# Transposing k once, copying its exchanged halves, and moving sums and loads between engines in a scheduled attention and feed-forward kernel

## The chip, the cores and the metric

One Trainium2 chip, one core. The engines are TensorE (PE; its weight loads are shown apart as PEld), VectorE (DVE), ScalarE (ACT), GpSimd (POOL) and SyncE (SP, which only issues transfers). The metric is device time of one execution in microseconds. The median of three timed executions of the kernel before is 986.57 us (986.48, 986.57, 989.59).

## The reference

Block-causal attention (8 batches, 8 heads, 576 positions of 64, blocks of 64: a position sees its own block and all earlier ones), then a feed-forward layer on its output:

```python
scores = scale * np.matmul(q, k.transpose(0, 1, 3, 2))
mask = block_i >= block_j
scores = np.where(mask, scores, -1000000000.0)
attn = np.exp(scores - np.max(scores, axis=-1, keepdims=True))
attn = attn / (np.sum(attn, axis=-1, keepdims=True) + 1e-09)
out = np.matmul(attn, v)
h = x @ w_in                      # x: 4608 x 512, w_in: 512 x 2048
g = h * np.clip(h + 3.0, 0.0, 6.0) / 6.0
return g @ w_out                  # w_out: 2048 x 512
```

Inputs and outputs are float32.

## The kernel before

Work is split into 32 pairs of heads (n = 0 to 31, four to a batch) and 13 pieces of positions for the feed-forward layer (up to 384 columns, 16 hidden tiles each). The first four pairs and the first piece are computed in f32 (names ending in 32, h0, o0), while the weights are loaded, scaled and split. From pair 4 on every f32 operand is split into two f16 parts, hi and lo, scaled by powers of two; a product is then three f16 products, hi hi, hi lo and lo hi, except for scores, where all parts of q meet all of k.

For scores, `qk_prep` takes a pair's q and k (positions on partitions), finds their maxima (`qkmx`), from these a power-of-two scale (`rs_q`, by way of a small matmul `mb_q`), writes scaled hi parts and residues into `qks`, and one transposing transfer on SyncE's queue turns `qks` into `qkT` (head dimension on partitions). `qkT` has three planes: plane 0 has q's hi on the lower 64 partitions and lo on the upper; planes 1 and 2 have k arranged so that the two products of plane 0 with each add up to all four combinations. In the kernel before, plane 1 holds k's hi on both halves and plane 2 its lo on both, so hi and lo are each written twice into `qks` (the second time by a copy that may run on VectorE, GpSimd or ScalarE) and three planes of nine 128-wide blocks are transposed: twenty-seven blocks.

`s_group` does the scores of three blocks of rows (groups g = 0, 1, 2): matmuls `s`, maxima `st`, exponentials `p` on ScalarE, normalised hi and lo parts `phl`, and transposing transfers `pT<-phl` on SyncE (8 blocks for group 0, 18 for group 1, 8, 8 and 10 for group 2). `pv_group` (two per pair) multiplies `pT` by v's parts `vhl` and writes piece buffers `x`. Then `ffn1_` gives hidden tiles h (two PSUM banks; in the last two pieces by products `m` of sums of halves), r and g, and `ffn2_` accumulates o; `osb` is stored.

The order is not that of the code: a recorder takes every operation with the engines that may run it, and a list scheduler (`schedule`) places them by a due time (`key`), estimated durations (`cost`), buffers, and two tables of numbers: `SHIFT` moves due times and `LEAN` moves the choice between engines. All recorded instructions therefore carry one line, L852, and are told apart by tiles. Each engine runs its list in order and waits where an operand is late. Loads may go on SyncE's or ScalarE's queue (`AQ`); stores and transposing transfers go on SyncE's. `pv_group32` spreads reciprocal row sums over a diagonal (`rd`), one block at a time.

Of the kernel before, what the change touches and what calls it, by code (L numbers as in the profile page):

```python
# [8 lines left out]
F16 = mybir.dt.float16  # L9
BF16 = mybir.dt.bfloat16  # L10
# [41 lines left out]
QKA = 8  # L52
RDW = "PA"
# [369 lines left out]
class Recorder:  # L423
# [165 lines left out]
    def cost(self, eng, method, args, kw, outs, ins):  # L589
# [40 lines left out]
        if eng == "gpsimd":  # L630
            if method == "memset":
                return 20 + 1.0 * n, 50 + n, False
            occ = 75 + (2.0 if method == "tensor_tensor" else 1.1) * n
            return occ, occ + 30, True
# [1479 lines left out]
```

## Time and profile before

| | |
|---|---|
| median of three executions | 986.57 us |
| profiled execution | 993.96 us |
| its span, first to last instruction | 992.2 us |
| mean granted TensorE clock | 0.994 |
| TensorE busy | 969.3 us (98%) |
| weight loads busy | 699.9 us (71%) |
| VectorE busy | 882.7 us (89%) |
| ScalarE busy | 637.2 us (64%) |
| GpSimd busy | 68.4 us (7%) |
| mean DMA rate | 130 GB/s, 129.03 MB |

In the rows, the columns of the stretch table are: stretch and its length, busy time and instruction count of PE, PEld, DVE, ACT and POOL, granted TensorE clock, DMA share and GB/s. Waits read "who waited <- for whom: us in total, times, longest". Timeline rows give start, duration, engine, operation, tiles (written <- read), count, and in brackets idle time before with what ended it; ACTq and SPq are the engine's issuing of a transfer. A tile's rows give minimum/median/maximum duration in ns, first and last start, and the time from issue to landing of its transfers. Group rows end with busy us, mean ns, and idle time before.

### The profile page before, as it was taken

How to read it: one execution, taken by the hardware profiler on the slowest of the kernel's cores; microseconds unless marked ns; L12 is line 12 of the kernel's file. 1: busy time of each engine (PE TensorE's matmuls, PEld its weight loads, DVE VectorE, ACT ScalarE, POOL GpSimd, SP SyncE). 2: the span in 40 equal slices, each digit the busy share in tenths (PEclk: the TensorE clock that was granted, in tenths of full speed). 3: DMA queues.
4: the chain of work that ended last, by engine and by line, in shares of the span. 5: the costliest groups of instructions: out<-in, count | busy, mean ns of one | idle time of the engine just before them, and what ended most of it. 6: DMA issues, size and time to landing. Idle time of an engine off the chain costs nothing.

```text
span 992.2 us, 31091 instructions
## 1 busy us (share of the span) xinstructions
PE 969.3 (98%) x12585; PEld 699.9 (71%) x12585; DVE 882.7 (89%) x2443; ACT 637.2 (64%) x1539; POOL 68.4 (7%) x237
## 2 busy tenths in 40 slices
PE   6999999999999999999999989999999999999998
PEld 5666667777778776687666767777767666768785
DVE  6999999999999999999997968988988879987864
ACT  4788868676767775887785756664757644443422
POOL 1132200000000000000000000000000100000000
PEclk9999999999999999999999989999999999999999
DMA  8974468989969779998996876584877462000000
GB/s 235 314 214 146 97 122 150 177 135 189 180 101 211 139 150 177 158 187 151 172 174 111 136 143 122 105 171 100 130 147 107 84 125 36 2 34 2 34 3 32
DMA packets 407184, 129.03 MB, mean 130 GB/s; under 512 B 393984, under 2 KB 396544, under 8 KB 407040
## 3 DMA queue, kind: packets, MB, share of 16 engines
q1 hardware_dynamic: 351232, 107.26, 57.8%
q10 hardware_dynamic: 55808, 19.78, 8.9%
q8 instruction: 98, 1.61, 0.7%
q14 instruction: 46, 0.38, 0.1%
HBM read 45.09 MB, written 9.44 MB: 55 GB/s over the span
## 4 chain that ended last, share of the span: by engine, by line
PE 51%; ACTq 1%; DVE 1%; ACT 1%; issue 0%
PE o L852 23%; PE h L852 16%; PE m L852 6%; PE s L852 3%; PE pv L852 3%; ACTq L852 1%; ACT osb L852 0%; DVE qks L852 0%; ACT p L852 0%; DVE st L852 0%; DVE x L852 0%; ACT r L852 0%; DVE r L852 0%; DVE osb L852 0%; DVE g L852 0%
## 5 line engine op out<-in xcount | busy, mean ns | idle before, releaser
L852 PE MATMUL o<-wout,g 128*64 128x512 f16 (+3 forms) x3336 | 405.2, 379 | 0.0
L852 PE MATMUL h<-x,win 128*64 128x384 f16 (+2 forms) x3952 | 357.8, 320 | 2.6 <-DVE r L852 2.0
L852 PEld LDWEIGHTS <-win 128*64 128x64 f16 (+1 forms) x4440 | 258.3, 110 | 74.0 <-issue 5.7
L852 PEld LDWEIGHTS <-g 128*64 128x64 f16 x3360 | 206.7, 110 | 119.5 <-issue 1.4
L852 ACT ACTIVATE p<-s,st,esc 128x384 f32<-128x384 f32 (+4 forms) x280 | 163.3, 588 | 61.1 <-DVE st L852 38.0
L852 ACT ACTIVATE r<-h,eg,sh 128x384 f32<-128x384 f32 (+1 forms) x192 | 111.5, 600 | 73.8 <-PE h L852 61.8
L852 DVE SCALAR_TENSOR_TENSOR phl<-p,st,phl 128x384 f16<-128x384 f32 (+4 forms) x252 | 137.1, 586 | 0.2
L852 DVE TENSOR_REDUCE st<-s 128x1 f32<-128x384 f32 (+4 forms) x280 | 117.9, 446 | 11.8 <-PE s L852 11.5
L852 DVE SCALAR_TENSOR_TENSOR r<-r,eg,h 128x384 f32<-128x384 f32 (+1 forms) x160 | 93.0, 585 | 19.6 <-ACT r L852 19.0
L852 DVE SCALAR_TENSOR_TENSOR g<-r,g 128x384 f16<-128x384 f32 (+1 forms) x192 | 101.2, 533 | 9.1 <-ACT g L852 8.2
L852 ACT ACTIVATE g<-r 128x384 f16<-128x384 f32 (+1 forms) x140 | 70.5, 506 | 57.3 <-PE o L852 27.8
L852 PE MATMUL s<-qkT 128*64 128x512 f16 (+7 forms) x1120 | 98.1, 289 | 4.4 <-ACT p L852 4.3
L852 ACT ACTIVATE phl<-p,st 128x384 f16<-128x384 f32 (+4 forms) x149 | 78.5, 567 | 36.3 <-DVE st L852 21.0
L852 PEld LDWEIGHTS <-qkT 128*64 128x64 f16 x1120 | 60.0, 111 | 28.7 <-issue 7.6
L852 PEld LDWEIGHTS <-vhl 128*64 128x64 f16 x1680 | 71.9, 110 | 10.0 <-issue 1.5
L852 PE MATMUL pv<-pT,vhl 128*64 128x192 f16 (+2 forms) x1680 | 72.9, 233 | 0.9 <-DVE x L852 0.5
L852 POOL MEMSET p<- 128x64 f32 x140 | 22.3, 159 | 546.5 <-DVE phl L852 482.9
L852 ACT ACTIVATION_READ_ACCUMULATOR p<-s,st,esc 128x1 f32 x280 | 55.4, 198 | 0.0
L852 ACT ACTIVATE r<-hf,eg,sh 128x192 f32<-128x192 f32 (+1 forms) x48 | 26.2, 592 | 44.0 <-DVE hf L852 42.5
L852 DVE SCALAR_TENSOR_TENSOR qks<-qk,rs_q,qks 128x576 f16<-128x576 f32 x56 | 44.4, 807 | 0.1
L852 DVE TENSOR_SCALAR phl<-p,st 128x128 f16<-128x128 f32 (+4 forms) x103 | 40.1, 414 | 1.0
L852 PE MATMUL m<-x,ws 128*64 128x192 f16 x768 | 37.9, 246 | 0.0
(191 smaller groups left out, 1028.9 us busy)
## 6 DMA issues: line engine op xcount, KB each, us to landing
out_dram<-osb SPq DMA_DIRECT2D x34, 256.0 KB, 2.4
qk<-in_q_dram SPq DMA_DIRECT2D x20, 288.0 KB, 4.8
vnat<-in_v_dram ACTq DMA_DIRECT2D x42, 128.0 KB, 4.2
rawo<-in_moe_w_out_dram SPq DMA_DIRECT2D x9, 512.0 KB, 6.1
qk<-in_k_dram ACTq DMA_DIRECT2D x16, 288.0 KB, 5.7
qk<-in_k_dram SPq DMA_DIRECT2D x12, 288.0 KB, 4.2
vnat<-in_v_dram SPq DMA_DIRECT2D x22, 128.0 KB, 3.5
x<-in_moe_w_in_dram SPq DMA_DIRECT2D x5, 512.0 KB, 7.2
```

The source lines that it names most:

```text
L852: getattr(eng, method)(*args, **kw)
```

## The change

- `qk_prep`: k is written as two halves (lo below, hi above) and transposed as one plane, so `qks` has two planes and the transposition eighteen blocks. Plane 2 of `qkT` is then plane 1 with its halves exchanged, made by two transfers from one half of the partitions to the other on SyncE's queue. The two copies into `qks` fall away.
- `QKA` goes from 8 to 32: for every pair ScalarE may give the scale's input, as two sums of absolute values, where VectorE gives one pass of maxima. (`VMG = 99` leaves the same choice for v off.)
- `RDW`: the three spreadings of a group's row sums become one operation of 192 columns, on VectorE or GpSimd instead of GpSimd or ScalarE.
- Loads of v, q and k from the ninth pair on (`n < 2 * NPAIR` no longer holds) go only on SyncE's queue.
- `cost`: estimated GpSimd durations are raised; both tables have new numbers throughout.

```diff
--- before.py
+++ after.py
@@ -49,8 +49,9 @@
 BQ = ("sync", "scalar")
 OQ = ("sync",)
 GRM = 3
-QKA = 8
-RDW = "PA"
+QKA = 32
+RDW = ("vector", "gpsimd")
+VMG = 99
 
 NMIN = 64
 LANES = 8
@@ -76,324 +77,306 @@
 
 
 SHIFT = {
-    0: 41, 2: 284, 3: -222, 4: 16, 5: -43, 6: -115, 7: 119, 8: 168, 11: -88, 12: 152, 13: 20, 14: -246,
...
+    0: -73, 2: 127, 3: -91, 4: 197, 5: 202, 6: -33, 7: 232, 8: -21, 11: 71, 12: 190, 13: 80, 14: 82, 15: 150,
...
 }
 LEAN = {
-    20: (-1038, 0), 50: (1191, 0), 60: (179, 0), 70: (-42, 0), 80: (0, -166), 110: (-195, 0), 111: (-195, 0),
...
+    20: (154, 0), 21: (49, 0), 50: (307, 0), 80: (0, 17), 81: (403, 0), 111: (68, 0), 140: (-69, 0),
...
 }
 
 
@@ -630,7 +613,7 @@
         if eng == "gpsimd":
             if method == "memset":
                 return 20 + 1.0 * n, 50 + n, False
-            occ = 75 + (2.0 if method == "tensor_tensor" else 1.1) * n
+            occ = 75 + (2.6 if method == "tensor_tensor" else 1.3) * n
             return occ, occ + 30, True
         f32 = mybir.dt.size(ins[0].dtype) == 4
         occ = max(n / 2.37, 26) * (4 if f32 else 1) + 2
@@ -1154,10 +1137,12 @@
         full = (NJ - 1) * P
         for h in range(2):
             nc.load(
-                t[:, :NJ - 1, h, :], v[b, 2 * hp + h, :full].rearrange("(j p) d -> p j d", p=P), AQ
+                t[:, :NJ - 1, h, :], v[b, 2 * hp + h, :full].rearrange("(j p) d -> p j d", p=P),
+                AQ if n < 2 * NPAIR else OQ,
             )
         nc.load(
-            t[:BLK, NJ - 1, :, :], v[b, 2 * hp:2 * hp + 2, full:].rearrange("h p d -> p h d"), AQ
+            t[:BLK, NJ - 1, :, :], v[b, 2 * hp:2 * hp + 2, full:].rearrange("h p d -> p h d"),
+            AQ if n < 2 * NPAIR else OQ,
         )
 
     def v_max(n):
@@ -1168,7 +1153,13 @@
             ab = ab[:, :NJ * 2 * D].rearrange("p (j h d) -> p j h d", h=2, d=D)
             nc.scalar.activation(ab, vnat[n % NVB], AF.Abs, accum_out=vmax[b][:, hp:hp + 1])
         else:
-            absmax(vmax[b][:, hp:hp + 1], vnat[n % NVB], AX.XYZ)
+            ways = [("vector", "tensor_reduce", (vmax[b][:, hp:hp + 1], vnat[n % NVB]),
+                     dict(axis=AX.XYZ, op=ALU.max, apply_absolute_value=True))]
+            if n >= VMG:
+                ab = sm.tile([P, NJ, 2, D], BF16, tag="vs", bufs=1, name=f"va{n}")
+                ways.append(("scalar", "activation", (ab, vnat[n % NVB], AF.Abs),
+                             dict(accum_out=vmax[b][:, hp:hp + 1])))
+            nc.add(ways)
         if hp == NPAIR - 1:
             m1 = sm.tile([P, 1], F32, tag="vm1", name=f"vm1_{b}")
             nc.vector.tensor_reduce(m1, vmax[b], axis=AX.X, op=ALU.max)
@@ -1207,18 +1198,19 @@
         for s, src in enumerate((q, k)):
             nc.load(
                 t[:, s],
-                src[b, 2 * hp:2 * hp + 2].rearrange("h s d -> (h s) d").rearrange("(t p) d -> p t d", p=P), AQ,
+                src[b, 2 * hp:2 * hp + 2].rearrange("h s d -> (h s) d").rearrange("(t p) d -> p t d", p=P),
+                AQ if n < 2 * NPAIR else OQ,
             )
         qn[n] = t
 
     def qk_prep(n):
         t = qn.pop(n)
         mx = sm.tile([P, 2], F32, tag="qkmx", name=f"qkmx{n}")
-        sp = attp.tile([P, 3, NST, 2, D], F16, tag="qks", name=f"qks{n}", bufs=1)
+        sp = attp.tile([P, 2, NST, 2, D], F16, tag="qks", name=f"qks{n}", bufs=1)
         ways = [("vector", "tensor_reduce", (mx, t), dict(axis=AX.XY, op=ALU.max, apply_absolute_value=True))]
         if n < QKA:
             ways.append(("scalar", [
-                ("activation", (sp[:, 2].rearrange("p t l d -> p (t l d)")[:, :NST * D].rearrange("p (t d) -> p t d", d=D), t[:, s], AF.Abs), dict(accum_out=mx[:, s:s + 1]))
+                ("activation", (sp[:, 1].rearrange("p t l d -> p (t l d)")[:, :NST * D].rearrange("p (t d) -> p t d", d=D), t[:, s], AF.Abs), dict(accum_out=mx[:, s:s + 1]))
                 for s in range(2)
             ]))
         nc.add(ways)
@@ -1230,21 +1222,21 @@
         esc[n] = sc
 
         nc.scaled(sp[:, 0, :, 0], t[:, 0], rs[:, 0:1], "AV")
-        nc.scaled(sp[:, 1, :, 0], t[:, 1], rs[:, 1:2], "AV")
+        nc.scaled(sp[:, 1, :, 1], t[:, 1], rs[:, 1:2], "AV")
         nc.vector.scalar_tensor_tensor(
             sp[:, 0, :, 1], t[:, 0], rs[:, 0:1], sp[:, 0, :, 0], op0=ALU.mult, op1=ALU.subtract
         )
         nc.vector.scalar_tensor_tensor(
-            sp[:, 2, :, 0], t[:, 1], rs[:, 1:2], sp[:, 1, :, 0], op0=ALU.mult, op1=ALU.subtract
+            sp[:, 1, :, 0], t[:, 1], rs[:, 1:2], sp[:, 1, :, 1], op0=ALU.mult, op1=ALU.subtract
         )
-        for c in (1, 2):
-            nc.scaled(sp[:, c, :, 1], sp[:, c, :, 0], 1.0, "VPA")
         o = attp.tile([P, 3, 2 * S], F16, tag="qkT", name=f"qkT{n}")
         nc.sync.dma_start(
-            o.rearrange("p c (t x) -> p (c t) x", x=P),
+            o[:, :2].rearrange("p c (t x) -> p (c t) x", x=P),
             sp.rearrange("p c t l d -> p (c t l d)"),
             transpose=True,
         )
+        for h in range(2):
+            nc.load(o[h * BLK:(h + 1) * BLK, 2], o[(1 - h) * BLK:(2 - h) * BLK, 1], OQ)
         qkT[n] = o
 
 
@@ -1404,8 +1396,8 @@
         nc.vector.tensor_scalar(r, r, 1e-9, 1.0, op0=ALU.add, op1=ALU.mult)
         nc.vector.reciprocal(r, r)
         rd = sm.tile([P, GB, BLK], F32, tag="rd", bufs=2, name=f"rd{n}_{g}")
-        for i in range(GB):
-            nc.scaled(rd[:, i], ident2, r[:, i:i + 1], RDW)
+        eye, rr = ident2.unsqueeze(1).to_broadcast([P, GB, BLK]), r.unsqueeze(2).to_broadcast([P, GB, BLK])
+        nc.add([(e, "tensor_tensor", (rd, eye, rr), dict(op=ALU.mult)) for e in RDW])
         if g == 0 or PRO:
             o = 2 if g else len(n_ev) % 3
             pr = ps_o.tile([P, GT], F32, tag=f"o{o}", name=f"pr{n}_{g}")
```

The order moves everywhere; three places are shown. The number after a name's group is a buffer number; the digits in `p23_0`, `s23_0` are pair and block or group.

**ScalarE, the exponentials of pair 23's first group.** `vnat` and `qk` are v, q and k as loaded, `r7` and `g7` hidden tiles of piece 7, `x1` a piece buffer, `vhl23` v's parts of pair 23. Before:

```order
L852 ACTIVATE vhl23_1751<-vnat3_103,rs_v5_1503 128x5x128
L852 ACTIVATE r7_0_1586<-h7_0_1585,eg8_723,sh4_8_1587 128x384
L852 DMA qk25_1795<-in_k_dram 128x9x64
L852 ACTIVATE x1_82<-pv22_0_1710 128x192
L852 DMA vnat3_103<-in_v_dram 128x4x64 x2
L852 DMA vnat3_103<-in_v_dram 64x2x64
L852 ACTIVATE r7_3_1619<-h7_3_1618,eg8_723,sh4_8_1587 128x384
L852 ACTIVATE p23_0_1714,st23_0_1712<-s23_0_0_0_1713,st23_0_1712,esc23_1675 128x64
L852 ACTIVATE p23_1_1715,st23_0_1712<-s23_0_0_0_1713,st23_0_1712,esc23_1675 128x128
L852 ACTIVATE g7_3_1620<-r7_3_1619 128x384
```

After:

```order
L835 ACTIVATE phl22_7_1704<-p22_7_1698,st22_2_1696 128x4x128
L835 ACTIVATE r7_2_1603<-h7_2_1602,eg8_723,sh4_8_1587 128x384
L835 ACTIVATE x1_82<-pv22_0_1710 128x192
L835 ACTIVATE p23_0_1714,st23_0_1712<-s23_0_0_0_1713,st23_0_1712,esc23_1675 128x64
L835 ACTIVATE p23_1_1715,st23_0_1712<-s23_0_0_0_1713,st23_0_1712,esc23_1675 128x128
L835 ACTIVATE p23_2_1716,st23_0_1712<-s23_0_0_0_1713,st23_0_1712,esc23_1675 128x192
L835 ACTIVATE r7_3_1619<-h7_3_1618,eg8_723,sh4_8_1587 128x384
L835 ACTIVATE phl23_0_1717<-p23_1_1715,st23_0_1712 128x128
L835 ACTIVATE g7_3_1620<-r7_3_1619 128x384
```

The four loads that stood ahead of `p23` on ScalarE are gone from its list.

**SyncE, around pair 24's transposition of q and k.** `pT23` are the transposed probabilities of pair 23, `out_0_dram` a store. Before:

```order
L852 DMA qk25_1795<-in_q_dram 128x9x64
L852 DMA_TRANSPOSE qkT24_1732<-qks24_1726 128x27x128
L852 DMA_TRANSPOSE pT23_0_1711<-phl23_0_1717 128x8x128
L852 DMA_TRANSPOSE pT23_0_1711<-phl23_1_1740 128x18x128
L852 DMA_TRANSPOSE pT23_1_1752<-phl23_6_1760 128x8x128
L852 DMA_TRANSPOSE pT23_1_1752<-phl23_7_1761 128x8x128
L852 DMA_TRANSPOSE pT23_1_1752<-phl23_8_1762 128x10x128
L852 DMA vnat4_104<-in_v_dram 64x2x64
```

After:

```order
L835 DMA_TRANSPOSE qkT24_1732<-qks24_1726 128x18x128
L835 DMA_TRANSPOSE pT23_0_1711<-phl23_0_1717 128x8x128
L835 DMA qk25_1795<-in_q_dram 128x9x64
L835 DMA qk25_1795<-in_k_dram 128x9x64
L835 DMA qkT24_1732<-qkT24_1732 64x1152 x2
L835 DMA_TRANSPOSE pT23_0_1711<-phl23_1_1740 128x18x128
L835 DMA vnat4_104<-in_v_dram 128x4x64 x2
```

The transposition has eighteen blocks instead of twenty-seven, and the two copies of `qkT24` stand after one short transposition and two loads, ahead of the eighteen-block transposition of pair 23 and of the loads of v.

**VectorE, at the first f16 hidden tiles (h1, in r1).** `rsio` is the scale of the last weight chunk, `win` and `wout` the weight splits that use it, `st4` maxima of pair 4, `r1_0` and `r1_1` the step that frees a bank of the hidden tiles. Before:

```order
L852 RECIPROCAL rsio_88<-pwio_87 128x2
L852 TENSOR_REDUCE st4_2_604<-s4_2_1_0_607 128x1
L852 TENSOR_SCALAR win_85<-x2_83,rsio_88 128x2x256
L852 TENSOR_REDUCE st4_2_604<-s4_2_1_1_608 128x1
L852 SCALAR_TENSOR_TENSOR win_85<-x2_83,rsio_88,win_85 128x2x256 x2
L852 SCALAR_TENSOR_TENSOR r1_1_601<-r1_1_601,eg5_588,h1_1_600 128x384
L852 SCALAR_TENSOR_TENSOR r1_0_585<-r1_0_585,eg5_588,h1_0_584 128x384
L852 SCALAR_TENSOR_TENSOR wout_86<-x3_84,rsio_88,wout_86 128x512
```

After:

```order
L835 RECIPROCAL rsio_88<-pwio_87 128x2
L835 TENSOR_TENSOR pp8_721<-pwio_87 128x8
L835 TENSOR_REDUCE st4_1_572<-s4_1_2_0_577 128x1
L835 TENSOR_SCALAR win_85<-x2_83,rsio_88 128x2x256
L835 TENSOR_SCALAR st4_1_572<-st4_1_572,esc4_471 128x1
L835 SCALAR_TENSOR_TENSOR win_85<-x2_83,rsio_88,win_85 128x2x256 x2
L835 TENSOR_SCALAR st4_1_572<-st4_1_572 128x3
L835 SCALAR_TENSOR_TENSOR wout_86<-x3_84,rsio_88,wout_86 128x512
L835 SCALAR_TENSOR_TENSOR r1_0_585<-r1_0_585,eg5_588,h1_0_584 128x384
```

One more weight split stands ahead of the first of the r1 rows. On TensorE, the next hidden tile that needs a freed bank followed the last matmuls of `h1_1` at once; in the new order four scores of pair 4 and the last f32 output tiles `o0` stand in between:

```order
L835 LDWEIGHTS qkT4_472
L835 MATMUL s4_2_1_1_608<-qkT4_472 64x512
L835 MATMUL o0_1_295<-x3_84,g0_15_560 64x256 x2
L835 MATMUL o0_0_294<-x3_84,g0_15_560 128x512
L835 LDWEIGHTS win_85
L835 MATMUL h1_1_600<-x1_82,win_85 64x384
```

The row of `h1_1` is now the one that needs the freed bank.

610 rows, old and new, of tables (LEAN, SHIFT) are left out of this document.

## The prediction

> **What bounds the kernel now.** I read the engines' shares first, then the stretches of 25 us in which TensorE falls short, then who it waited for, then the instructions around its two longest waits inside the program.
>
> ```profile
> PE 969.3 (98%) x12585; PEld 699.9 (71%) x12585; DVE 882.7 (89%) x2443; ACT 637.2 (64%) x1539; POOL 68.4 (7%) x237
> ...
> 0.00:25.00 25.00, 17.38 (x230) 13.65 (x232) 15.43 (x46) 11.18 (x39) 4.49 (x26) 1.00 0.88 236
> 25.00:50.00 25.00, 22.77 (x245) 15.77 (x243) 22.73 (x66) 19.96 (x59) 3.15 (x6) 1.00 0.95 314
> 100.00:125.00 25.00, 24.01 (x221) 15.96 (x219) 23.86 (x71) 19.43 (x48) 5.49 (x10) 1.00 0.49 96
> 125.00:150.00 25.00, 22.97 (x234) 15.87 (x235) 23.23 (x79) 17.91 (x46) 1.90 (x6) 0.93 0.65 122
> 575.00:600.00 25.00, 20.89 (x214) 13.72 (x212) 15.83 (x47) 10.29 (x28) 0.54 (x4) 0.86 0.70 114
> 975.00:1000.00 25.00, 13.57 (x126) 8.59 (x122) 4.38 (x9) 3.44 (x6) 0.00 (x0) 0.95 0.09 31
> ...
> PE s L852 <- ACT p L852: 4.3, 2, 4.1
> PE pv L852 <- DVE x L852: 0.5, 1, 0.5
> ```
>
> TensorE is busy 969.3 of 992.2 us, so 22.9 us is all that any change to the other engines can take from its idle time. Its instructions are the same in number before and after. The shortfall sits in the first 150 us (7.6 in the first stretch, 2.2 in the second, 1.0 and 2.0 further on), in the stretch 575 to 600 (4.1), and at the end (3.6 of the 17.2 us left). Of waits after 150 us the list has, beside the 4.1 us one, nothing above 0.5 us. So between 150 and 990 us VectorE's 89% and ScalarE's 64% are paid for by TensorE's own work, and relieving them is worth nothing there.
>
> The stretch 575 to 600:
>
> ```profile
> 575.28 6.33 SPq L852 DMA_TRANSPOSE qkT<-qks  x1
> 576.67 7.21 ACTq L852 DMA_DIRECT2D vnat<-in_v_dram  x3
> 583.93 0.67 ACT L852 ACTIVATE r<-h,eg,sh 128x384 f32<-128x384 f32 x1 [6.99 <-issue]
> 586.38 0.85 PE L852 MATMUL s<-qkT 128*64 128x384 f16 x4 [4.11 <-ACT p L852]
> ...
> L852 ACTq DMA_DIRECT2D vnat<-in_v_dram x56: 372/457/3772, 0.7 to 665.3; - x56
> ```
>
> While SyncE's 6.33 us transposition was being issued, ScalarE spent 7.21 us on issuing three loads of v that take 0.457 us each in the median. The exponentials behind them came late, and TensorE stood 4.11 us. Then its granted clock fell: 0.86 over 25 us is 3.5 us lost. Together 7.6 us. This matters for the reference point. The profiled execution took 993.96 us, of which 1.8 us lie outside its span of 992.2; the three timed executions are 986.48, 986.57 and 989.59. 993.96 less 7.6 is 986.4: the median run shows no such stall. I therefore sum from 986.6, as an execution without it, and its removal is worth 0 against the median though 7.6 against the profiled one.
>
> **The change part by part.** *Loads leave ScalarE.* From the ninth pair on 66 loads (14 of k, 7 of q, 45 of v) go from ScalarE's queue to SyncE's. At the 0.457 us above that is 30 us of ScalarE's queue, under TensorE's cover: 0. Lost cover is priced by the row itself, 7.6 us a time.
>
> [...]
>
> *k transposed once.* Per pair two copies of half planes go, and a third of the transposition.
>
> ```profile
> L852 DVE TENSOR_SCALAR qks<-qks x32: 281/301/482, 106.8 to 790.5; 128x576 f16<-128x576 f16 x32
> L852 ACT ACTIVATE qks<-qks x20: 666/678/687, 106.4 to 789.7; 128x576 f16<-128x576 f16 x20
> L852 SPq DMA_TRANSPOSE qkT<-qks x28: 4073/5382/7081, 107.1 to 790.9; - x28
> ...
> qkT<-qks SPq DMA_TRANSPOSE x28, 8.5
> ...
> L852 SPq DMA_DIRECT2D out_dram<-osb x39: 332/382/1296, 140.3 to 989.6; - x39
> DMA to landing us min/median/max: 1.7/2.4/4.9
> ...
> L852 SPq DMA_TRANSPOSE pT<-phl x1: 2407/2407/2407, 782.1 to 782.1; - x1
> DMA to landing us min/median/max: 6.3/6.3/6.3
> ...
> L852 SPq DMA_TRANSPOSE pT<-phl x1: 3192/3192/3192, 814.1 to 814.1; - x1
> DMA to landing us min/median/max: 5.2/5.2/5.2
> ```
>
> VectorE loses 32 x 0.30 = 9.6 us, ScalarE 20 x 0.68 = 13.6 us. The new transposition has eighteen blocks, and so has the second one of each pair's probabilities; the last two rows are two of those: 2.4 to 3.2 us to issue, 5.2 to 6.3 to land, against 5.4 and 8.5 for twenty-seven blocks. Two copies of 144 KB follow it. Their nearest rows are the output's stores on the same queue, up to 256 KB: 0.38 us to issue, 1.7 to 4.9 to land; I take the median, 2.4. Scores therefore get k's second arrangement at 5.8 + 0.4 + 2.4 = 8.6 us (7.9 to 11.1) instead of 8.5, and the first one 2.7 earlier: 0.
>
> The copy, however, is a wait in SyncE's order. Behind the issue of a transposition SyncE reaches it after whatever stands between: for pair 24 a short transposition and two loads, for pair 30 nothing, where it then stands 5.2 - 3.2 to 6.3 - 2.4 = 2.0 to 3.9 us. Queued behind are the transpositions of the probabilities, and the pv matmuls wait for those.
>
> How much room they have: the transposition at 782.1 above landed at 788.4, and the thirteenth of these matmuls needs it.
>
> ```profile
> 788.72 1.17 PE L852 MATMUL pv<-pT,vhl 128*64 128x192 f16 x30
> 970.89 17.68 PE L852 MATMUL o<-wout,g 128*64 128x512 f16 x162
> ```
>
> That one starts at 788.72 + 12 x 0.039 = 789.2: room 0.8 us. Reading the 28 pairs alike gives a median of 4.7 us, and eight under 3.0. The new order also brings the pv matmuls nearer: counted in columns at the pace of the second row (17.68 us for 162, 109 ns for 512), TensorE's work between the last scores of a pair's second group and the pv that needs them falls from 18.2 to 16.1 us in the median (least: 12.9 to 11.5), and for the third group from 26.7 to 23.5. Less work on VectorE (36 us of 883) and shorter transpositions give some of it back. Bounds: 0, if the latency falls as far; 7 us, if 3 us of room go for good (the sum of the shortages of those eight). I take +0.5, near the first, since every one of the 56 pv groups still has room in the trace.
>
> *Sums on ScalarE.* 20 of 24 maxima of q and k leave VectorE, two sums each on ScalarE.
>
> ```profile
> L852 DVE TENSOR_REDUCE qkmx<-qk 128x2 f32<-128x1152 f32 x24 | 32.2, 1343 | 0.3 <-DMA qk<-in_k_dram 0.3
> L852 ACT ACTIVATE qks<-qk x8: 667/686/687, 96.1 to 168.8; 128x576 f16<-128x576 f32 x8
> L852 ACT ACTIVATION_READ_ACCUMULATOR qks<-qk x8: 185/188/205, 96.6 to 169.3; 128x1 f32 x8
> L852 POOL TENSOR_SCALAR rd<-ident,sums 128x64 f32<-128x64 f32 x13 | 7.8, 609 | 33.9 <-DVE sums L852 27.3 <-PE pt L852 6.5
> L852 ACT ACTIVATE rd<-ident,sums 128x64 f32<-128x64 f32 x23 | 6.6, 341 | 0.8 <-POOL rd L852 0.5 <-DVE sums L852 0.3
> 20.73 0.36 DVE L852 TENSOR_TENSOR x<-pf,rb 128x192 f32<-128x192 f32 x1 [0.24 <-PE pf L852]
> ```
>
> VectorE -20 x 1.34 = -27 us, ScalarE +40 x (0.69 + 0.19) = +35, which its lost copies and load issues (14 + 30) outweigh: 0, inside TensorE's cover. *Merged row sums:* three spreadings of 0.34 to 0.61 us become one, of 0.36 us by the nearest row, ten times on VectorE and twice on GpSimd. No wait of TensorE names it: 0, with -1 to +1 us for the first 125 us, where VectorE takes 10 x 0.36 us more.
>
> *The new order at 138 us.* The first f16 hidden tiles wait there for a bank.
>
> ```profile
> 134.23 0.19 PE L852 MATMUL mb_w<-dg_w,one 2*64 2x2 bf16 x2
> 136.62 0.15 DVE L852 TENSOR_SCALAR am_w<-mb_w 128x2 f32<-128x2 f32 x1
> 138.61 1.40 DVE L852 SCALAR_TENSOR_TENSOR win<-x,rsio,win 128x512 f16<-128x512 f32 x2
> 139.93 1.13 DVE L852 SCALAR_TENSOR_TENSOR r<-r,eg,h 128x384 f32<-128x384 f32 x2
> 140.59 0.68 PE L852 MATMUL h<-x,win 128*64 128x384 f16 x6 [2.03 <-DVE r L852]
> 140.98 0.74 DVE L852 SCALAR_TENSOR_TENSOR wout<-x,rsio,wout 128x512 f16<-128x512 f32 x1
> ```
>
> The wait is 2.03 us, and the clock of 0.93 in that stretch costs a further 1.75. In the new order TensorE has 0.6 us more work (two f32 output tiles and four scores) ahead of the next hidden tile, and VectorE one more split of 0.74 us less 0.2 of reductions ahead of r, but VectorE takes up the last weight scale earlier: 2.2 us after TensorE's sum for it in the first two rows, 1.1 us by the durations of the rows that the new order leaves in between. So 2.03 + 0.5 - 0.6 - 1.1 = 0.8; without the last term 1.9. I take 1.3, a gain of 0.7 (bounds: 2.0 gained, 1.0 lost), and half of the clock's loss, 0.9 (bounds 0 and 1.75).
>
> [...]
>
> Sum: 986.6 + 0 + 0 + 0.5 + 0 + 0 - 0.7 - 0.9 = **985.5 us**. Within 0.3% (2.96 us), about what a measurement of this kernel can tell from no change, that is no change.
>
> **The rivals.** *Both early losses go, and half of the other waits between 25 and 125 us* (2.2 + 0.5 + 0.5 + 1.0 = 4.2): -2.0 - 1.75 - 2.1 gives 980.7. For it: the new order has cover at the place, and shorter chains. Against it: VectorE is 93% busy there, and gets more to do.
>
> ```profile
> 50.00:75.00 25.00, 24.49 (x223) 15.97 (x222) 22.87 (x65) 20.56 (x48) 7.63 (x9) 1.00 0.70 211
> 75.00:100.00 25.00, 24.52 (x229) 15.28 (x227) 24.10 (x64) 22.93 (x59) 7.01 (x11) 1.00 0.47 142
> ```
>
> *SyncE stands at the copies.* The probabilities' transpositions behind them land up to 3 us later, and pv matmuls with room under that make TensorE wait: +7, so 993.5. It decides once the loss of room passes 0.8 us. For it: room of 0.8 us at pair 30, whose copy follows its transposition at once. Against: most copies have transpositions or loads between.
>
> *ScalarE's stall moves to SyncE.* All loads now share the transpositions' queue; one that holds SyncE for 7.2 us as it held ScalarE makes a pv 7.2 - 4.7 = 2.5 us late, with 1.75 of clock: 990.8. For it: the 7.21 us row. Against: one such stall among 56 loads, and none in the median.
>
> *The change doesn't do what it says* I exclude: the order shows 66 loads, 20 maxima and all 56 copies moved.
>
> **How the numbers follow.** No change 0.42 (985.5, its own range 983.7 to 989.0), both early losses gone 0.36 (980.7), copies 0.17 (993.5), stall on SyncE 0.05 (990.8). Hence faster 0.36, same 0.42, slower 0.22. The range reaches to 980.0, just past the faster case, and to 991.0, between the two slower ones; outside lie half the copies' chance and a tenth below.
>
> **What would show it.** Right: no wait of ScalarE for its own issuing after 150 us, no TensorE wait over 1 us after 150 us, first 150 us of TensorE within 2 us of before, a wait of 0.8 to 1.9 us for DVE r near 138 us. For the copies: pv among TensorE's waits by some 0.5 to 2 us at several pairs, SyncE waiting for qkT's landing. For the faster case: PEclk 1.00 between 125 and 150. Wrong altogether: TensorE's busy time itself changing by more than 2 us.

## The result, and the profile after

The changed kernel took 1002.03 us in the median of 6 executions (1000.19 to 1003.93), the kernel before 990.48 in the median of 6 (986.48 to 992.9; the three shown at first are among them). The ratio is 1.0121, 95% interval 1.0098 to 1.0143: slower by 11.6 us by the medians and 12 by the ratio, outside the range of the prediction. The profiled execution took 1003.25 us, its span is 1001.4, its mean granted clock 0.995.

The engines' shares, some of the stretches (columns as before) and some of TensorE's waits in the changed kernel:

```profile
PE 973.6 (97%) x12585; PEld 720.3 (72%) x12585; DVE 871.2 (87%) x2435; ACT 636.7 (64%) x1560; POOL 43.9 (4%) x204
...
25.00:50.00 25.00, 21.09 (x177) 13.28 (x176) 21.30 (x58) 15.89 (x47) 2.36 (x4) 0.86 0.79 247
75.00:100.00 25.00, 22.57 (x212) 14.67 (x214) 22.65 (x58) 21.41 (x49) 2.65 (x5) 1.00 0.48 141
125.00:150.00 25.00, 24.58 (x243) 15.31 (x244) 24.16 (x75) 17.73 (x45) 0.78 (x5) 1.00 0.54 99
300.00:325.00 25.00, 22.24 (x376) 18.21 (x372) 21.25 (x66) 15.67 (x40) 0.61 (x3) 0.96 0.95 183
575.00:600.00 25.00, 23.89 (x289) 16.61 (x287) 22.42 (x64) 14.47 (x36) 1.07 (x6) 1.00 0.90 175
...
PE s L835 <- ACT p L835: 3.6, 3, 2.8
PE pf L835 <- ACT pf L835: 2.2, 2, 1.9
PE pv L835 <- ACT p L835: 1.4, 2, 1.1
PE pv L835 <- ACT x L835: 1.3, 3, 0.4
PE h L835 <- DVE r L835: 0.6, 1, 0.6
```

Two places that the prediction named came out better: the stretch 575 to 600, 20.89 busy before, is at 23.89, and the stretch 125 to 150 is at 24.58 with a full clock (22.97 and 0.93 before). What was not there before: a start with a clock of 0.86 (25 to 50 us), longer waits between 75 and 100 us, 2.8 us of idle time near 320 us, and several waits of `s` and `pv` for ScalarE, where the kernel before, after 150 us, had one of 4.1 us and otherwise nothing above 0.5. TensorE waits for ScalarE, whose share of busy time is the same 64% as before.

### The profile page after: what moved, and what is told of

The parts are those of the page before. It is cut to its first block, busy times and chain, and to the rows that moved or that the text cites. A ratio compares the mean times of both kernels' runs of the same rounds, so it can differ in the third digit from the quotient of the medians.

```text
span 1001.4 us, 31119 instructions
## 1 busy us (share of the span) xinstructions
PE 973.6 (97%) x12585; PEld 720.3 (72%) x12585; DVE 871.2 (87%) x2435; ACT 636.7 (64%) x1560; POOL 43.9 (4%) x204
## 5 line engine op out<-in xcount | busy, mean ns | idle before, releaser
L835 PE MATMUL o<-wout,g 128*64 128x512 f16 (+2 forms) x3336 | 403.9, 379 | 0.0
L835 PEld LDWEIGHTS <-win 128*64 128x64 f16 (+1 forms) x4440 | 267.8, 110 | 63.8 <-issue 3.8
L835 PEld LDWEIGHTS <-g 128*64 128x64 f16 x3360 | 217.2, 110 | 111.2 <-issue 0.4
L835 ACT ACTIVATE p<-s,st,esc 128x384 f32<-128x384 f32 (+3 forms) x280 | 162.7, 586 | 66.3 <-DVE st L835 50.5
L835 DVE SCALAR_TENSOR_TENSOR phl<-p,st,phl 128x256 f16<-128x256 f32 (+4 forms) x252 | 137.5, 582 | 1.0 <-ACT phl L835 0.7
L835 DVE TENSOR_REDUCE st<-s 128x1 f32<-128x384 f32 (+2 forms) x280 | 118.0, 448 | 7.2 <-PE s L835 6.8
L835 PE MATMUL s<-qkT 128*64 128x64 f16 (+7 forms) x1120 | 98.0, 288 | 3.9 <-ACT p L835 3.6
L835 ACT ACTIVATE phl<-p,st 128x128 f16<-128x128 f32 (+4 forms) x145 | 76.9, 567 | 25.3 <-DVE st L835 12.8
L835 PEld LDWEIGHTS <-vhl 128*64 128x64 f16 x1680 | 72.8, 110 | 12.1 <-issue 5.0
L835 DVE TENSOR_SCALAR phl<-p,st 128x512 f16<-128x512 f32 (+4 forms) x107 | 41.6, 413 | 1.8
L835 ACT ACTIVATE qks<-qk 128x576 f16<-128x576 f32 x48 | 32.6, 679 | 6.8 <-DMA qkT<-qks 5.1
```

What stands on the lines that cost most here:

```text
L835: getattr(eng, method)(*args, **kw)
```

## Experiments

All ratios below are to the kernel before, timed beside it on the same chip (medians 990.2 to 992.1), with 95% intervals; a thousandth is about 1 us. The runs were spread over four chips, so they are compared by these ratios. To separate the operations from their order, the planner's answer was replaced in all these kernels by a written list of operations with their engines, so that the order of one kernel could be given to the operations of another:

```diff
     def emit(self):
-        for o in self.schedule():
-            eng = getattr(self.nc, o.eng)
-            for method, args, kw in o.ways[o.eng][0]:
-                getattr(eng, method)(*args, **kw)
+        for x in ORDER:
+            o = self.ops[x // 5]
+            o.eng = self.NAMES[x % 5]
+            for method, args, kw in o.ways[o.eng][0]:
+                getattr(getattr(self.nc, o.eng), method)(*args, **kw)
```

### The operations or their order

First theory: the new order costs, at the start and at 320 us. Second: the changed operations cost, by the copies in SyncE's queue.

The changed operations in the old order, maxima on the engines of before (the lines show the copies; the merged row sums and the later loads on SyncE are in it too):

```diff
 ORDER of before, per pair
 SyncE     DMA_TRANSPOSE qkT<-qks
-VectorE   TENSOR_SCALAR qks<-qks
-ScalarE   ACTIVATE qks<-qks
+SyncE     DMA qkT<-qkT
+SyncE     DMA qkT<-qkT
```

> The changed operations (k transposed once, two copies on SyncE, merged row sums, later loads on SyncE alone), put in the order of the kernel before; each copy stands some 6 us behind its transposition, and the maxima of q and k stay on the engines of before, because in that order ScalarE's sums would need a tile that the pair before still holds. If the new order is what costs (theory 1), this is within 3 us of the kernel before, and up to 7 us faster where ScalarE's stall near 580 us was in that run. If the changed operations cost, through copies in SyncE's queue and thinner room (theory 2), it is 8 to 12 us slower than before, with pv among TensorE's waits.

Measured: 989.61 us, 0.9996 (0.9979 to 1.0012).

The old operations in the new order (the same lines with - and + exchanged; maxima, row sums and loads go back with them):

> The operations of before (k transposed twice, its copies on the engines, maxima on the engines of before, three spreadings for the row sums, later loads on both queues) in the order of the changed kernel. Theory 1: 8 to 12 us slower than before, with TensorE's waits near 26 and 29 us, a half clock behind them, and the wait near 320 us. Theory 2: within 3 us of before.

Measured: 1042.58 us, 1.0533 (1.0498 to 1.0568).

The start of the old order, then what is left in the new one (`ORDER = old[:375] + rest(new)`):

> The changed kernel with the first 375 of its 6372 operations in the order of before (up to some 50 us), the rest in its own order. Theory 1, with two places of loss, 6 us by 50 us (two waits of 0.8 and 1.2 us near 26 and 29 us and the clock behind them) and 5 us at 320 us: 5 to 6 us faster than the changed kernel, so about 1.005 to 1.007 of before. Theory 2: as slow as the changed kernel, 1.010 to 1.014 of before.

Measured: 999.04 us, 1.0107 (1.0070 to 1.0143).

The reverse (`ORDER = new[:376] + rest(old)`):

> The changed operations with the first 376 in the order of the changed kernel, the rest in the order of before (the maxima of q and k from there on the engines of before). Theory 1: the early loss alone, 4 to 7 us slower than the run with all of its operations in the order of before. Theory 2: no difference between those two.

Measured: 998.94 us, 1.0100 (1.0070 to 1.0130), 10 us above the first run's 0.9996.

The first two seem to settle it for the order. Only the first, though, came as the first theory has it; the second misses its 8 to 12 us by 40, and the other two miss as well. The old operations in the new order lose four times what the changed kernel loses, so that order must rest on something that was taken out with them; and the first run leaves out one of the changed operations, ScalarE's sums, so it doesn't clear them all. The new start costs 1.4 us in the changed kernel (third run, within the intervals nothing) and 10 in the old order (fourth). The stretches 25 to 75 us of the first run and of the fourth show where these 10 us are:

```profile
25.00:50.00 25.00, 22.61 (x247) 15.73 (x244) 23.52 (x68) 18.47 (x50) 3.88 (x7) 1.00 0.97 308
50.00:75.00 25.00, 24.29 (x221) 16.15 (x222) 23.57 (x65) 19.77 (x43) 6.69 (x8) 1.00 0.70 206
```

```profile
25.00:50.00 25.00, 22.23 (x206) 14.37 (x206) 21.99 (x62) 16.44 (x49) 2.18 (x4) 0.86 0.80 244
50.00:75.00 25.00, 21.31 (x197) 13.88 (x194) 17.66 (x48) 15.41 (x34) 3.53 (x5) 0.80 0.80 251
```

The granted clock is 0.86 and 0.80: 8.5 us lost (0.14 and 0.20 of 25), while the busy time differs little in the first stretch. In the second it is 3.0 us lower: TensorE waits 3.7 us there for ScalarE's `pf`. Mean granted clocks were 0.987 to 0.993 in that kernel's executions, 0.998 to 1.000 in the first run's, 0.994 to 0.998 in the changed kernel's.

### The places in the changed kernel

Three places were looked at in the new order: the start (above, the third run), one near 584 us and one near 320 us. Near 584 us ScalarE's sums wait for a transfer; here are three instructions in order of time (start, duration, engine, what it does, in brackets the idle time ahead of it and who ended it), and the group of these sums with its idle time:

```profile
581.69 0.68 ACT L835 ACTIVATE qks<-qk 128x576 f16<-128x576 f32 x1 [1.44 <-DMA qkT<-qks]
583.74 0.77 ACT L835 ACTIVATE p<-s,st,esc 128x512 f32<-128x512 f32 x1
584.65 0.53 PE L835 MATMUL pv<-pT,vhl 128*64 128x192 f16 x12 [1.11 <-ACT p L835]
...
L835 ACT ACTIVATE qks<-qk 128x576 f16<-128x576 f32 x48 | 32.6, 679 | 6.8 <-DMA qkT<-qks 5.1
```

The sums write their by-product into the tile `qks`, of which there is one, and the transposition of the pair before may still be reading it. That wait could be read from the diff, which gives the tile one buffer (`bufs=1`) and has the sums write into it; the profile of before, where only eight early sums did so, could not show its price. The edit:

```diff
+        ab = attp.tile([P, NST, D], F16, tag="qab", name=f"qab{n}", bufs=1)
...
-                ("activation", (sp[:, 1]..., t[:, s], AF.Abs), dict(accum_out=mx[:, s:s + 1]))
+                ("activation", (ab, t[:, s], AF.Abs), dict(accum_out=mx[:, s:s + 1]))
```

> The changed kernel in its own order; ScalarE's sums for the maxima of q and k write their by-product to a tile of their own instead of the tile qks, which the transposition of the pair before still reads. Theory 3, that ScalarE's new wait for that transposition (1.44 us near 581 us of the changed kernel's profile, TensorE behind it 1.11 us) is one of the costs: ScalarE no longer waits for qkT's landing, the pv wait near 584 us goes, and the time falls by 1 to 3 us against the changed kernel. The rival, that these waits only take the place of others: within 1 us of the changed kernel.

Measured: 997.16 us, 1.0059 (1.0033 to 1.0085), 6 us better than the changed kernel by the ratios and twice what was expected. ScalarE no longer waits for the transposition, and the stretch 575 to 600 is full:

```profile
575.00:600.00 25.00, 25.00 (x315) 17.89 (x312) 22.52 (x71) 16.11 (x41) 1.07 (x6) 1.00 1.03 187
```

That the tile costs the 6 us is shown by the edit; where all of them lie is not: ScalarE's waits for the transposition are four, 5.1 us in all, and TensorE's wait behind the one at 584 us is 1.1 us.

Near 320 us ScalarE stands for a buffer:

```profile
313.58 0.76 SPq L835 DMA_DIRECT2D out_dram<-osb  x1
318.40 0.91 ACT L835 ACTIVATE r<-h,eg,sh 128x192 f32<-128x192 f32 x2 [2.86 <-DMA out_dram<-osb]
322.66 0.71 PE L835 MATMUL s<-qkT 128*64 128x384 f16 x4 [2.76 <-ACT p L835]
```

ScalarE's `r` shares the four `stage` buffers with the output's `osb`; the store of one had been issued 4.8 us earlier and had not landed. The edit gives the tag a fifth buffer (`NGB, NPB, NST_B = (4, 5, 5)` in place of `(4, 5, 4)`).

> The changed kernel in its own order, with five buffers instead of four for the tiles of the tag stage (ScalarE's r and the output's osb share them). Theory 1 at its second place, that ScalarE waits 2.9 us near 316 us for a buffer whose store has not landed, TensorE 2.8 us behind it, and its clock another 1.7: that wait goes, 4 to 5 us faster than the changed kernel. The rival, that ScalarE is late there for another reason (the three loads of v that SyncE issues meanwhile): the wait stays, within 1 us.

Measured: 1002.11 us, 1.0108 (1.0079 to 1.0138), 1 us better than the changed kernel by the ratios instead of 4 to 5.

Then both edits together:

> Both edits together, the tile of its own for ScalarE's sums and the fifth buffer of stage. If the two are separate costs, their gains add up: 5 to 8 us faster than the changed kernel, 1.003 to 1.007 of before; what is then left is the start (waits and half clock before 40 us). If not, no faster than the better of the two.

Measured: 997.39 us, 1.0057 (1.0032 to 1.0082), no better than the tile alone, although it lies in the 1.003 to 1.007 of the first case: the tile gives all of it. With five buffers the wait near 320 us shrinks, as expected, from 2.8 to 1.0 us, but the gain did not come. The weights at the start use the same buffers, and the profile of the run with the fifth buffer alone shows a lower clock there:

```profile
25.00:50.00 25.00, 22.35 (x160) 14.65 (x160) 19.24 (x53) 14.20 (x41) 2.17 (x4) 0.73 0.79 243
300.00:325.00 25.00, 24.01 (x417) 19.55 (x415) 22.95 (x73) 17.25 (x44) 0.61 (x3) 1.00 0.96 187
```

24.01 busy instead of 22.24 in the second row, and a clock of 0.73 instead of 0.86 in the first: 1.8 and 1.0 gained (idle time and clock), 3.3 lost. The mean clocks of that kernel's executions, 0.991 to 0.996, lie mostly below the changed kernel's 0.994 to 0.998.

The later loads back on their old queues, order unchanged (`AQ` in all three places of the code):

> The changed kernel in its own order, with the loads of the later pairs on the queues that they had before (69 of 120 again on ScalarE's). If the loads on SyncE delay the output's stores and the probabilities' transpositions (theory 2 for this part), the wait near 320 us goes or halves and the time falls by 3 to 5 us. If they are not the cause, within 2 us of the changed kernel, or slower by up to 7 us where ScalarE stands at an issue again.

Measured: 1003.64 us, 1.0117 (1.0083 to 1.0152): the loads are not what costs. In the new order they gain nothing on SyncE's queue either.

### One part at a time, in the old order

The first run again, with the fifth buffer of `stage`:

> As the run with the changed operations in the old order (maxima on the engines of before), with five buffers of stage instead of four. That run's profile shows one wait of 3.3 us near 231 us, VectorE's osb standing 3.5 us for a buffer whose store had not landed, and 1.7 us of clock behind it. Theory 1, that a new order costs through single places like this one: the wait goes, 3 to 5 us faster than that run (about 985), below the kernel before. Rival: the fifth buffer changes the start, where weights use the same buffers, and a half clock there (3 to 7 us) takes the gain.

Measured: 988.98 us, 0.9975 (0.9959 to 0.9992), 2 us better than the first run instead of 3 to 5. VectorE's wait for a store near 231 us went, and TensorE then waited at the same place for the second copy of k, 2.7 us, which SyncE had issued 3.9 us after the first:

```profile
226.86 1.78 SPq L913 DMA_DIRECT2D qkT<-qkT  x1
230.79 0.58 SPq L913 DMA_DIRECT2D qkT<-qkT  x1
234.43 0.50 PE L913 MATMUL s<-qkT 128*64 128x64 f16 x10 [2.69 <-DMA qkT<-qkT]
```

The first run left ScalarE's sums out. With them, in the old places of the maxima:

```diff
 ORDER of before, 20 of 24 pairs
-VectorE   TENSOR_REDUCE qkmx<-qk
+ScalarE   ACTIVATE qab<-qk, READ_ACCUMULATOR, twice
```

> All of the change in the old order, ScalarE's sums too (20 of the 24 later maxima on ScalarE, as in the changed kernel, their by-product in a tile of its own). If the sums cost only by their wait for qkT's transposition: within 2 us of the run with the changed operations but the old maxima (989.6). If the 35 us that they add to ScalarE cost by themselves: 3 to 6 us slower than it, with TensorE waiting for ScalarE's p or x.

Measured: 997.19 us, 1.0065 (1.0041 to 1.0089): 7 us slower than the first run. The sums cost by themselves, in the old order too, and although the copies and the later loads have left ScalarE in this kernel.

The three places of the changed kernel taken away together (`old[:375] + rest(new)`, the tile `qab`, five buffers):

> The changed kernel with its three places taken away together: the first 375 operations in the old order, a tile of its own for ScalarE's sums, five buffers of stage. If these three are what it loses (3 at the start, 4 to 5 by the sums' waits, 3 to 5 at 320 us): 990 to 993, level with before. If the new order costs by many small waits beyond them: 994 to 998.

Measured: 994.85 us, 1.0038 (1.0022 to 1.0055): the second case, so the three places are not all that the changed kernel loses.

One part alone, the loads, in the kernel before:

```diff
 ORDER of before, 69 loads
-ScalarE   DMA vnat<-in_v_dram
+SyncE     DMA vnat<-in_v_dram
```

> The kernel before in its own order, with one part of the change alone: the later loads of v, q and k (69 that stood on ScalarE's queue) on SyncE's, each at its old place. By the prediction's term this is worth 0 against the median and 7 us against an execution with ScalarE's stall near 580 us; since 3 of 6 and later most runs of before lie at 990 to 993, I now expect 1 to 4 us faster than before. Rival: the stall moves to SyncE, same or slower.

Measured: 986.53 us, 0.9952 (0.9933 to 0.9971). The loads alone are a gain of 4.8 us in the old order, and the fastest kernel so far. (69 loads are all of ScalarE's from the ninth pair on; the prediction's 66 is the net change in its list.) The stretch 575 to 600:

```profile
575.00:600.00 25.00, 24.58 (x338) 17.95 (x335) 21.10 (x62) 16.84 (x41) 1.59 (x7) 1.00 0.68 125
```

Then the sums taken out of the new order (`qkmx` back on VectorE, at the same places):

> The changed kernel in its own order, with the 20 later maxima that ScalarE summed back on VectorE; all else as changed. In the old order ScalarE's sums cost 7.6 us, and in the new one their wait for qkT's transposition 4.9. If the sums cost as much whatever the order: 5 to 12 us faster than the changed kernel, 990 to 997. If the new order has been laid around them, so that VectorE's 27 us more now come in its way: slower than the changed kernel, 1003 to 1030 (the operations of before in the new order took 1042.6).

Measured: 1017.91 us, 1.0275 (1.0240 to 1.0310). Taking the sums back makes it slower: in the new order VectorE has no room for them, and now TensorE waits for VectorE:

```profile
PE h L913 <- DVE r L913: 6.5, 9, 2.0
```

So the new order and the sums belong together. That explains part of the 1042.6 us of the old operations in that order; the 25 us between the two runs were not taken apart.

The first run once more, the two copies of a pair next to each other and 1 us earlier:

> The changed operations in the old order with the old maxima, as in the first run of that kind, but both copies of each pair stand together, 1 us earlier, so that nothing comes between them on SyncE. That run lost 3.1 us against the loads alone; its profile, and that of its variant with five buffers, show one place near 230 us (a buffer whose store had not landed, or a wait of 2.7 us for the second copy, issued 4 us after the first). If the copies and the merged row sums cost nothing but such places: 985 to 988, level with the loads alone. If SyncE's standing at the copies thins the room of the probabilities' transpositions: 990 to 994, with pv among TensorE's waits.

Measured: 988.34 us, 0.9981 (0.9965 to 0.9997), 3 us behind the loads alone, between the two cases, and with no wait of `pv` over 0.4 us.

Then one part each time on top of the loads, in the old order; first the sums (as above, without copies and merged row sums):

> The kernel before in its own order with two parts of the change: the later loads on SyncE, and ScalarE's sums for 20 of the 24 later maxima (by-product in a tile of its own, each at the old place of the maximum). Against the loads alone (986.5): 5 to 9 us slower, about 994, if the sums cost by themselves what they cost beside the copies (7.6); within 2 us, if it was the copies and the sums together.

Measured: 994.57 us, 1.0040 (1.0024 to 1.0055): 8.7 us behind the loads alone.

The merged row sums (`rd` as one `tensor_tensor` at the place of the first of the three):

> The kernel before in its own order with the later loads on SyncE and the merged row sums. Their profile in the first 75 us shows waits of TensorE some 1.5 us longer than with the loads alone. If that is the merging's: 1 to 2 us slower than the loads alone, 987.5 to 988.5. If it is chance: within 0.7 us of 986.5.

Measured: 986.08 us, 0.9951 (0.9932 to 0.9969): the merged row sums are free.

K transposed once, the two copies next to each other and early:

> The kernel before in its own order with the later loads on SyncE and k transposed once (the two copies together on SyncE, some 5 us behind the transposition's start). If the copies are what the last run of this kind lost against the loads alone (1.8 us): 987.5 to 989. If they are free: 985.5 to 987, and with them the prediction's term of +0.5 stands.

Measured: 988.79 us, 0.9974 (0.9959 to 0.9990): k's single transposition costs 2.2 us, about the width of the intervals.

| on top of before, old order | ratio | step |
|---|---|---|
| later loads on SyncE | 0.9952 | -4.8 us |
| and merged row sums | 0.9951 | -0.1 |
| and k transposed once, instead | 0.9974 | +2.2 |
| and ScalarE's sums, instead | 1.0040 | +8.7 |
| the four steps added | 1.0061 | +6.0 |
| all four, measured | 1.0065 | +6.5 |
| all four in the new order, sums with a tile of their own | 1.0059 | +5.9 |
| the changed kernel: the same with the shared tile | 1.0121 | +12.1 |

("Instead" stands for: on top of the loads alone.) The steps, measured in the old order, add up within their intervals (some 0.002 each), and the new order with the same parts comes to the same time; the shared tile is the rest. That does not make each step the same in the new order: there the loads are worth nothing (1.0117 with them back on ScalarE, 1.0121 without), and taking the sums out costs 15 us. The sums' step was measured with the copies still on ScalarE; with the copies gone it was 6.9 us (1.0065 against the first run's 0.9996).

How a sum costs shows at 186 us, first with the loads alone, then with the sums (same columns as above):

```profile
185.09 0.67 ACT L914 ACTIVATE r<-h,eg,sh 128x384 f32<-128x384 f32 x1
185.97 0.73 ACT L914 ACTIVATE p<-s,st,esc 128x448 f32<-128x448 f32 x1 [0.21 <-DVE st L914]
187.23 1.27 PE L914 MATMUL pv<-pT,vhl 128*64 128x192 f16 x30
```

```profile
184.88 0.67 ACT L914 ACTIVATE r<-h,eg,sh 128x384 f32<-128x384 f32 x1
185.44 0.67 ACT L914 ACTIVATE qab<-qk 128x576 f16<-128x576 f32 x1
186.24 0.68 ACT L914 ACTIVATE qab<-qk 128x576 f16<-128x576 f32 x1
186.92 0.71 ACT L914 ACTIVATE p<-s,st,esc 128x448 f32<-128x448 f32 x1
188.16 1.07 PE L914 MATMUL pv<-pT,vhl 128*64 128x192 f16 x21 [1.04 <-ACT p L914]
```

ScalarE had 0.21 us of idle time between `r` and `p`. The two sums with their reads take 1.5 us there, the exponential starts at 186.92 instead of 185.97 although all else runs 0.2 us earlier, and TensorE's `pv`, which takes its PSUM bank from the same three as the scores `s` and needs the one that the exponential empties, stands 1.04 us. The same picture stands at 284, 323 and 380 us. In the whole of that kernel after 150 us:

```profile
PE pv L914 <- ACT p L914: 2.2, 2, 1.2
PE s L914 <- ACT p L914: 1.7, 2, 0.9
PE mt_v L914 <- ACT p L914: 1.0, 1, 1.0
```

None of these three rows is in the list of the loads alone, which has only:

```profile
PE pv L914 <- DVE x L914: 0.5, 1, 0.5
PE pv L914 <- ACT x L914: 0.4, 1, 0.4
```

Adding up from both traces, after 150 us, every gap of over 0.25 us between two matmuls (time from start to start, less the first one's columns at 0.21 ns each, the pace of 109 ns for 512, and less what a half clock takes) gives 11.5 us with the sums and 2.2 without: 9.3 us for a step of 8.7.

### The wait near 138 us

On top of the loads alone, `r` of one hidden tile goes ahead of the weight splits:

```diff
 ORDER, ScalarE
+ACTIVATE r1_1
 ACTIVATE win
-ACTIVATE r1_1
 ORDER, VectorE
+SCALAR_TENSOR_TENSOR r1_1
 SCALAR_TENSOR_TENSOR win
 SCALAR_TENSOR_TENSOR win
-SCALAR_TENSOR_TENSOR r1_1
```

> The kernel before with the later loads on SyncE, and two instructions moved at the wait near 138 us: ScalarE's r and VectorE's r of one hidden tile go ahead of the splits of the last weight chunk beside them. TensorE's wait of 2.0 us for DVE r becomes 0.6 to 1.0, and the half clock of 3.4 us behind it is rarer: 0 to 2.5 us faster than the loads alone (986.5). Rival: the splits, now 0.6 us later, are what TensorE waits for next: no gain.

Measured: 986.36 us, 0.9971 (0.9957 to 0.9985): no gain over the loads alone. TensorE's waits between 130 and 150 us:

```profile
PE h L914 <- DVE r L914: 1.4, 1, 1.4
PE mb_q L914 <- ACT p L914: 0.9, 1, 0.9
```

The wait fell from 2.0 to 1.4 us, not to 0.6 to 1.0, and another one of 0.9 us came behind it, for ScalarE's `p` and not for the splits that the rival named.

## Why the prediction was wrong

The step that failed is "*Sums on ScalarE* ... 0, inside TensorE's cover". That cover is a sum over 990 us, and what TensorE waits for is one exponential at one moment. Measured: +8.7 us in the old order, and still +6.9 with the copies and the later loads off ScalarE, so that what leaves ScalarE elsewhere does not pay for the sums. The balance itself was off too: load issues do not count as busy time (before, from 576.7 to 583.9 us, while three loads of v were being issued, ScalarE shows 0.24 us busy), and in the old order ScalarE is busy 621.6 us without the sums and 650.7 with them, against 637.2 before. In the changed kernel it comes to 636.7, but there the planner also took other work off ScalarE (21 scaled parts `qks<-qk,rs_q` instead of 30). None of these totals tells the cost. The sentence in the first part on which it rests, that ScalarE's 64% is paid for by TensorE's own work, is true of the kernel before; it says nothing of the room ahead of a single `p`, 0.21 us in the rows above.

The other points, in their order:

- **A step that was missing.** The change adds a wait: the sums write into `qks` and so stand behind the transposition of the pair before. It would have been found by asking of each new writer who still reads its tile, since `qks` has one buffer. It costs about 6 us. In the old order most of the 20 sums would stand ahead of that transposition (18 of these maxima start before it in the profile of before), so with the shared tile they could not keep their old places.
- **Loads leave ScalarE: 0.** Measured -4.8 us in the old order, and nothing in the new one. The reference point was wrong: three executions stood for the kernel, two of them at 986.5, and its later medians were 990.2 to 992.1. Subtracting the stall from one profiled execution and finding the result near the smallest times was taken as proof that the median has no stall. That the stall comes in some executions and not in others is likely from this, but only one trace of the kernel before exists, so it is argued and not shown.
- **k transposed once 0, copies +0.5.** Measured +2.2 together, inside the bounds of 0 to 7. The copies' landing, 2.4 us by the output's stores, is 3.4 in the changed kernel (first row), but 2.6 in the run that measured the 2.2 us (second row), so the landing does not explain them. Nor do they come in the way that was expected: after 150 us that run's new waits are mainly of `s` for ScalarE's `p`, four of 1.4 us in all, and none is of `pv` for a transposition. What causes them stays open.

```profile
qkT<-qkT SPq DMA_DIRECT2D x56, 144.0 KB, 3.4
qkT<-qkT SPq DMA_DIRECT2D x56, 144.0 KB, 2.6
```

- **Merged row sums 0** (-1 to +1): measured -0.1.
- **The new order at 138 us, -0.7 and -0.9.** In the changed kernel no wait is left ahead of that hidden tile, which starts at 146.86 us straight behind the f32 output tiles; one of 0.6 us for `r` comes at 151.6, ahead of the next, and the clock of the stretch 125 to 150 is 1.00. So 1.4 to 2.0 and 1.75 were won there, some twice what was predicted. The half of the clock's loss, 0.9, was an estimate between its two bounds, and no run shows it: the clock of that stretch was 0.93 in the traces of before and of the loads alone, and 1.00 in those of the changed kernel and of the copies placed early. What the prediction left open is the rest of that order. Its first 150 us have waits of 1.2 us of `mb_v` and 1.9 of `pf`, both for ScalarE's `pf`, and a clock of 0.86 in one stretch, and were not "within 2 us": TensorE is busy 133.7 of these 150 us, 136.1 before, and stands 6.8 us at half clock (0.50 granted, from 29.3 us on) instead of 3.4 (from 141.6).
- **The rivals.** The case of both early losses going did not come: one went and others took its place. SyncE standing at the copies (+7) was the right sign from another cause. Its mark, `pv` among the waits at several places, did appear, but it was ScalarE's `p` and `x` that these waited for, not a transposition; by the mark alone the wrong rival would have been confirmed. ScalarE's stall did not move to SyncE.
- **The signs.** That ScalarE waits for no issuing of its own held: it issues no load after 140 us. "No TensorE wait over 1 us after 150 us" failed by 2.8 and 1.1. "Wrong altogether: TensorE's busy time itself changing by more than 2 us" happened, 969.3 to 973.6.

The range missed because it was laid between the cases, and none of them had the sums cost anything: their term stood at 0 without bounds.

The best kernel found is the one before with the later loads on SyncE, with the merged row sums or without them: 986.1 to 986.5 us, 0.995 of before. Of the change, the loads are worth having in the old order, and the merged row sums are free.

## What to carry to other kernels

Do not balance an engine's work over the whole span: for each instruction that is moved onto an engine, find what stands behind it there at that moment, how much idle time lies ahead of that, and who waits for it. Ask of each new write, a by-product too, which earlier reader holds the tile. And where one of the first four executions lies 0.4 to 0.8% above the others, take the reference point from more of them; judge a part by doing it alone in an unchanged order.

## What the runs showed of the hardware

The same wait costs the clock or does not. TensorE's wait of 2.0 us near 138 us stands in the traces of the loads alone and of the copies placed early, with the same busy time in the stretch 125 to 150; the granted clock was 0.93 in the first and 1.00 in the second:

```profile
125.00:150.00 25.00, 22.97 (x234) 15.82 (x234) 23.23 (x80) 17.69 (x46) 1.91 (x6) 0.93 0.62 122
```

```profile
125.00:150.00 25.00, 22.97 (x255) 16.23 (x255) 24.78 (x83) 18.59 (x48) 2.19 (x8) 1.00 0.57 123
```

The two kernels differ in other places, and what decides was not shown. In the traces of before and of the changed kernel the granted clock was 0.50 for 3.41 us (before, from 141.6 us, behind the wait of 2.03; the changed kernel, from 322.9, behind the one of 2.76) or for 6.83 us (before, from 585.3, from inside the wait of 4.11 on; the changed kernel, from 29.3, behind one of 1.21). Out of one stretch of a single profile such half clocks took from 1.7 us (0.07 of 25, before) to 6.8 (0.27 of 25, the run with the fifth buffer alone), which is the size of most parts tried here.
